# Where the sums of weight blocks stand in a fused attention and two-product kernel: two moved ahead, twelve moved back, and another room for two blocks

## The chip, the cores and the metric

The kernel runs on one core of a Trainium2 chip. The metric is the device time of one execution in microseconds (us); the median of three executions of the kernel before is 661.0 us (659.6, 661.0 and 663.91). The core has a matrix engine (TensorE, PE in the profile; its weight loads are PEld), a vector engine (VectorE, DVE), an engine for activations and copies (ScalarE, ACT), GpSimd (POOL) and SyncE (SP). In this kernel POOL and SP mostly issue transfers (DMA). Each engine works through a list of its own, in order. Those lists are laid out when the program is built.

## The reference

A causal attention with decay, in blocks of 64 positions, gives a matrix x of 3072 x 512. Behind it stands a two-layer block without bias.

```python
for b in range(nb):                                   # attention, per block of 64
    intra = einsum('bhic,bhjc->bhij', qb, kb) * Dmask
    out[:, :, sl] = einsum('bhij,bhjd->bhid', intra, vb) + einsum('bhid,bhde->bhie', qb * lam_pow, kv_state)
    kv_state = lam_block * kv_state + einsum('bhsd,bhse->bhde', kb * rev_pow, vb)

x = attn_out.transpose(0, 2, 1, 3).reshape(B * S, H * D)   # (3072, 512)
h = x @ w_in                                               # (512, 2048)
g = h - np.tanh(h)
return g @ w_out                                           # (2048, 512)
```

There are 4 batches, 8 heads, 768 positions and a head size of 64. The weights come as 64-bit floats, the rest as 32-bit floats.

## The kernel before

**Groups.** The tokens are worked on in six groups (0 to 5) of 512: 128 positions of each of the four batches. A group has an attention part, a first product (x by `w_in`, called *up*), g = h - tanh(h), and a second product (g by `w_out`, called *down*). The 2048 columns of `w_in` are four *units* u of 512 columns. The 2048 rows of `w_out` are eight *row blocks* kt of 256 rows.

**Seven products in place of eight.** Matrices are cut in 2 x 2 quarters and multiplied with seven quarter products, numbered 1 to 7 (called P1 to P7), which need sums of quarters beforehand. `sums_in(u)` (L274) makes the sums of a unit of `w_in`: four vector operations on tiles of 128 x 512, three of them into `ws[u]`, one in place into `w1[u]`. `sums_out(kt)` (L282) makes the sums of a row block of `w_out`, four vector operations of 128 x 256, and sends the block to DRAM by POOL's queue (`factors`, `fine`); `sums_fine(u)` (L298) makes a second level of sums from two row blocks and sends those too. From group 1 on, the row blocks come back from DRAM in pieces `wb` (`piece`, L746), from a ring of seven. Some products are cut a second time: `inner_weights` (L660) makes, for P2 or P4 of the first product, the sums of quarters of a unit, four vector operations of 128 x 128, into a tile of a ring of four (tag "sums") and sends them to DRAM (`fine_in`) by POOL.

**Group 0 differs.** Its first product is plain (`up_plain`, L907; matmuls at L917), since the weights arrive only then. Each weight block comes as 64-bit words into `raw64`, and `round_block` (L308) turns it into 32-bit floats with three operations on ScalarE (L318 to L320) and two on the vector engine (L322, L323). `weights(n)` rounds the next blocks; a row block kt is two of these blocks. The turns over the units run with attention of group 1 in between. Behind the last turn comes the second product of group 0, a loop over kt in which `down_first(kt, ...)` (L938; matmuls at L947) runs all seven products for one row block, into seven PSUM banks that are kept through the whole loop. Products 6 and 3 of a step need `s24`, which `sums_late(kt)` (L951; L956 and L957) makes one step ahead; products 3 to 7 need the sums of `sums_out(kt)`. `first_results` (L959) empties the banks with one ScalarE operation and seven vector operations (L963 to L972). Then group 1 starts its first product with `up(1, 0, 1)` in the banks that become free (`up`, L601; matmuls at L610).

**Where the row blocks lie meanwhile.** Row blocks 0, 1, 4 and 5 take turns in the two rooms of the pool `wst`. Blocks 2, 3, 6 and 7 borrow `ws`, the room for the sums of `w_in`: each takes a third of `ws[3]` and all of `ws[2]` (blocks 2 and 6) or `ws[1]` (blocks 3 and 7). So the sums of unit 1 can be made only when row block 7 is through, and the sums of unit 0 can be made before. After the loop the pools `stage` (with `raw64` and the rounding's addends), `qpool` and `wst` are closed, and the pools `blk` (blocks of q and k for the transposes on the vector engine, L359) and `late` (the rings `wb` and "sums") take their place.

**Group 1.** In each unit the up products run in the order 2, 6, 5, 7, 1 of the next unit, 4, 3. `sums_in(2)` and `sums_in(3)` are in units 0 and 1. In the last unit the place of product 1 is taken by P1 of the second product (`down(1, 1)`, L792; matmuls at L803). `inner_weights` runs after each unit, for P2 and P4. `pieces(g, u)` puts parts of the next group's attention after each unit: transposes, scores (L448) and masks (L455).

**What sets the order.** The list of each engine is made by a planner that takes what is ready by its own estimate of times, the earlier in the program first. `tc.keep_in_program_order` (and `tied(True, ...)`) pins an operation behind the operation written before it on its engine. The sums in the loop over kt are all pinned, with two exceptions (`sums_out` of blocks 0 and 1); so are `att_sums(1)`, `sums_in`, `inner_weights`, the transposes and the rounding. The matmuls of `down_first` and `up` are not, and neither are the tanh, the copies and the sums in `up` (L618 to L650).

Of the kernel before, what the change touches and what calls it, by code (L numbers as in the profile page):

```python
# [24 lines left out]
def kernel(  # L25
# [225 lines left out]
    def weights(n):  # L251

        while ready["done"] < min(n, len(blocks)):
            at_ = ready["done"]
            load_weights(at_ + WAHEAD)
            kind, n_, m = blocks[at_]
            if kind == "out" and m == 0:
                pair[n_] = pair_tiles(n_)
            w = w1[n_][:, m] if kind == "in" else pair[n_][m][:, 0:2]
            if at_ in wraw:  # L260
                round_block(w, wraw.pop(at_))
            else:
                load_block(nc.gpsimd, w, kind, n_, m)
            ready["done"] += 1

    def pair_tiles(kt):

        if kt % 4 > 1:
            x, y = (ws[u].rearrange("p x k c -> p (x k) c") for u in (3, 4 - kt % 4))
            return x[:, ts(kt % 4 - 2, 2)], y[:, 0:6]  # L270
        wt = wst.tile([128, 8, 256], F32, name="wt", tag="w")
        return wt[:, 0:2], wt[:, 2:8]

    def sums_in(u):  # L274
        a11, a12, a21, a22 = (w1[u][:, 2 * c:2 * c + 2, r] for r, c in ((0, 0), (0, 1), (1, 0), (1, 1)))
        s1, s2, s4 = (ws[u][:, x] for x in range(3))
        for dst, x, y, op in ((s1, a21, a22, AL.add), (s2, s1, a11, AL.subtract), (a21, a11, a21, AL.subtract),
                              (s4, a12, s2, AL.subtract)):
            tc.keep_in_program_order(nc.vector.tensor_tensor(dst, x, y, op=op))
# [285 lines left out]
    def att_sums(g, bs=None):  # L565
        x0, x1 = xt[g, 0], xt[g, 1]
        b11, b21, b12, b22 = x0[:, 0:2], x0[:, 2:4], x1[:, 0:2], x1[:, 2:4]
        tt = xpool.tile([128, 3, 2, HB], F32, name="tt", tag="tt")
        tied(g == 1, nc.vector.tensor_tensor(tt[:, 0], b12, b11, op=AL.subtract))
        tied(g == 1, nc.vector.tensor_tensor(tt[:, 1], b22, tt[:, 0], op=AL.subtract))  # L570
        tied(g == 1, nc.vector.tensor_tensor(b12, b22, b12, op=AL.subtract))
        tied(g == 1, nc.vector.tensor_tensor(tt[:, 2], b21, tt[:, 1], op=AL.subtract))
        xt[g] = dict(B11=b11, B21=b21, B22=b22, T1=tt[:, 0], T2=tt[:, 1], T3=b12, T4=tt[:, 2])
# [86 lines left out]
    def inner_weights(u, ns=INNER):  # L660
        for n in ns:
            a11, a12, a21, a22 = (a_quarter(n, u, i, k) for i in range(2) for k in range(2))
            t = late["pool"].tile([128, 4, 128], F32, name="ws2", tag="sums", bufs=4)
            s1, s2, s4 = (t[:, x] for x in range(3))
            for dst, x, y, op in ((s1, a21, a22, AL.add), (s2, s1, a11, AL.subtract), (a21, a11, a21, AL.subtract),
                                  (s4, a12, s2, AL.subtract)):
                tc.keep_in_program_order(nc.vector.tensor_tensor(dst, x, y, op=op))
            nc.gpsimd.dma_start(out=fine_in[INNER.index(n)].rearrange("x p u c -> p u x c")[:, u], in_=t[:, 0:3])
# [283 lines left out]
    def sums_late(kt):  # L952
        u, m = divmod(kt, 2)
        g11, g21, s1 = (hidden(0, c)[:, u, m] for c in (11, 21, "S1"))
        s24[kt] = work.tile([128, 2, HB], F32, name="s24", tag="th")
        tc.keep_in_program_order(nc.vector.tensor_tensor(s24[kt][:, 0], s1, g11, op=AL.subtract))  # L956
        tc.keep_in_program_order(nc.vector.tensor_tensor(s24[kt][:, 1], g21, s24[kt][:, 0], op=AL.subtract))  # L957

    def first_results():  # L959
        flat = {n: t.rearrange("q m c -> q (m c)") for n, t in acc.items()}  # L960
        q, o11, q5, o12 = (otile(x) for x in ("q1", "o11", "q5", "o12"))
        nc.scalar.activation(q, flat[1], AF.Copy)
        tc.keep_in_program_order(nc.vector.tensor_tensor(o11, q, flat[2], op=AL.add))  # L963
        store(0, 11, o11)
        tc.keep_in_program_order(nc.vector.tensor_tensor(q, q, flat[6], op=AL.add))
        tc.keep_in_program_order(nc.vector.tensor_tensor(q5, q, flat[5], op=AL.add))
        tc.keep_in_program_order(nc.vector.tensor_tensor(q, q, flat[7], op=AL.add))
        tc.keep_in_program_order(nc.vector.tensor_tensor(o12, q5, flat[3], op=AL.add))
        store(0, 12, o12)
        tc.keep_in_program_order(nc.vector.tensor_tensor(q, q, flat[4], op=AL.add))  # L970
        store(0, 21, q)
        tc.keep_in_program_order(nc.vector.tensor_tensor(q5, q5, flat[7], op=AL.add))  # L972
        store(0, 22, q5)
# [48 lines left out]
    for u, cs, n0, n1, mid, more in turns:  # L1022
        turn = up_plain(u, cs)
        if n0:
            steps(turn, KI)
            run(mid)
            weights(ready["done"] + n0)
        every(turn)
        run(more)
        weights(ready["done"] + n1)  # L1030
        if cs[-1] == 22:
            sums_first(u)
            if u == 1:
                load_weights(NU * KI)
                load(2 * B)
                powers()
            if u == 2:
                sums_in(0)
    sums_out(0)
    sums_late(0)  # L1040
    att_out(1, P1, "att")
# [3 lines left out]
    for kt in range(KH):  # L1045
        down_first(kt, (1, 2, 5, 4, 7, 6, 3) if kt + 1 < KH else (1, 2, 6, 5, 7, 3, 4))
        if kt + 1 < KH:
            sums_late(kt + 1)
        if kt + 2 < KH:
            sums_out(kt + 2)  # L1050
        if kt in (0, 1, 3, 6):
            sums_fine((kt + 1) // 2)
        if 0 < kt and kt + 3 < KH:
            weights(ready["done"] + 2)
            load_weights(ready["done"] + WAHEAD)
        if kt == 5:
            att_sums(1)
    first_results()
    sums_in(1)
    early.close()  # L1060
    late["blk"] = ctx.enter_context(tc.tile_pool(name="blk", bufs=4))
    late["pool"] = ctx.enter_context(tc.tile_pool(name="late", bufs=1))
# [20 lines left out]
    for g in range(1, NG):  # L1083
        last = g == NG - 1
        for u in range(NU):
            for n in (2, 6, 5, 7, 1, 4, 3) if g < GI else (1, 7, 3) if u == 0 else (6, 5, 1, 7, 3) if u + 1 < NU else (
                    6, 5, 7, 1, 3):
                if n != 1:
                    up(g, u, n)
                elif u + 1 < NU:  # L1090
                    up(g, u + 1, 1)
                else:
                    if g == GI - 1:
                        inner_weights(u, INNER[:1])
                        pieces(g, u)
                    every(down(g, 1))
                if g == 1 and u < 2 and n == 5:
                    sums_in(u + 2)
            if g == GI - 1:
                inner_weights(u, INNER if u + 1 < NU else INNER[1:])  # L1100
            if g >= GI or u + 1 < NU:
                pieces(g, u)
        sums_twice(g, 4)
        sums_once(g, 11, "S1", 11)
        every(down(g, 2))
        sums_twice(g, 5)
        pieces(g, "P2")
        product = down_twice(g, 4, side(g, 1))
        steps(product, 4)
        pieces(g, "P4")  # L1110
        sums_once(g, 21, 21, 11)
        sums_twice(g, 6)
        every(product)
        product = down_twice(g, 5, side(g, 0))
        steps(product, 2)
        pieces(g, "P5")
        sums_twice(g, 7)
        every(product)
        product = down_twice(g, 6, side(g, 1))
        steps(product, 2)  # L1120
        if twice(g, 3):
            sums_twice(g, 3)
        every(product)
        pieces(g, "P6")
        every(down_twice(g, 7, side(g, 0)))
        if last:
            down_end(g)
            continue
        inner_tokens(g + 1)
        p3 = down_twice(g, 3, side(g, 1)) if twice(g, 3) else down(g, 3)  # L1130
        p2 = inner_steps(g + 1, 2, "ya")
        for n, (kind, _) in enumerate(in_turn(g)):
            next(p3 if kind == "down" else p2)
            pieces(g, ("inner", n))
        every(p2)
        every(p3)
        p4 = inner_steps(g + 1, 4, "yb")
        for at_, n in enumerate((None, None, 1, None, None, 6, None, None, 5, None)):
            if n is None:
                next(p4)  # L1140
            else:
                up(g + 1, 0, n)
            pieces(g, ("end", at_))
        every(p4)
        pieces(g, "end")
# [30 lines left out]
```

## Time and profile before

| | |
|---|---|
| median of three executions | 661.0 us |
| the profiled execution | 661.42 us |
| its span, first to last instruction | 659.6 us |
| VectorE busy | 486.4 us (74%) |
| ScalarE busy | 216.7 us (33%) |
| POOL busy | 200.6 us (30%) |
| DMA | 129.14 MB, 196 GB/s over the span |
| granted TensorE clock, mean | 1.000 |

One execution is profiled. A group of the profile names a line, an engine, an operation and the tiles (`out<-in`), with the shape as partitions x elements. A wait is idle time of an engine that ended when the named operation of another engine was done. Of the span, group 0's first product lies at about 22 to 91 us, its second product at 95.7 to 145.4, group 1's first product at 145.4 to 212 (with P1 of its second product at 195.4 to 202.3), and each later group takes some 104 us. In the loop over kt, TensorE takes about 6.05 us a step.

### The profile page before, as it was taken

The page shows a single profiled execution, that of the slowest core. Times are in us where ns is not written, and L with a number is a line of the kernel's source. Part 1 is how long each engine was busy: PE and PEld are TensorE (multiplying, and loading weights), DVE is VectorE, ACT ScalarE, POOL GpSimd, SP SyncE. Part 2 cuts the span into 40 slices and gives each one's busy share as a digit, 9 for nine tenths or more (in the row PEclk, how much of TensorE's full clock was granted, in tenths as well). Part 3 has the DMA queues.
Part 4 walks back from the last instruction along what each step waited for, and adds up shares of the span by engine and source line. Part 5 has one row for each costly group of instructions (what it writes and reads, how often), then busy time and mean ns, then how long its engine had stood idle before and what let it go on. Part 6 is the DMA issues. An engine that isn't in the chain of part 4 may idle for free.

```text
span 659.6 us, 14228 instructions
## 1 busy us (share of the span) xinstructions
PE 645.3 (98%) x5632; PEld 588.5 (89%) x5632; DVE 486.4 (74%) x869; ACT 216.7 (33%) x422; POOL 200.6 (30%) x349
## 2 busy tenths in 40 slices
PE   7899999999999999999999999999999999999997
PEld 6788988888788999988999988999988899988897
DVE  4576997997977876886877787787779687357563
ACT  4767773513231223232122243112223122334110
POOL 2000246773023554001445101355202354400250
PEclk9999999999999999999999999999999999999999
DMA  9988878999729676965578865587661677600481
GB/s 214 232 189 228 233 219 284 330 317 303 161 68 248 226 244 223 198 148 141 185 235 274 189 137 146 150 291 237 197 142 68 196 239 234 215 10 1 134 287 59
DMA packets 104818, 129.14 MB, mean 196 GB/s; under 512 B 63344, under 2 KB 80880, under 8 KB 104752
## 3 DMA queue, kind: packets, MB, share of 16 engines
q0 software_dynamic: 26400, 86.27, 41.2%
q1 hardware_dynamic: 78208, 41.96, 27.5%
q8 instruction: 45, 0.74, 0.5%
q14 instruction: 21, 0.17, 0.1%
q10 hardware_dynamic: 144, 0.00, 0.0%
HBM read 108.01 MB, written 20.19 MB: 194 GB/s over the span
## 4 chain that ended last, share of the span: by engine, by line
PE 79%; DVE 6%; DMA 6%; SPq 3%; issue 3%; ACT 1%; POOL 1%; DVEq 0%; POOLq 0%; ACTq 0%
PE y L610 15%; PE y L858 13%; PE zw L858 10%; PE z L610 9%; PE h L917 6%; PE y L803 5%; PE y L694 4%; PE w L803 4%; DMA k_blk<-in_k_dram 3%; PE z L694 2%; PE sp L448 2%; SPq L156 2%; PE acc L947 2%; DMA fine<-f 1%; PE op L484 1%
## 5 line engine op out<-in xcount | busy, mean ns | idle before, releaser
L767 POOL DMA_DIRECT2D wb<-fine x168 | 90.7, 540 | 156.7 <-PE y L858 53.0
L618 ACT ACTIVATE th<-g 128x512 f32<-128x512 f32 x76 | 47.5, 630 | 117.4 <-DVE g L623 48.9
L610 PE MATMUL y<-xt,w 128*128 128x256 f32 x320 | 74.0, 382 | 1.1 <-ACT g L638 1.1
L619 DVE TENSOR_TENSOR g<-g,th 128x512 f32<-128x512 f32 x76 | 52.4, 691 | 23.2 <-ACT th L618 22.8
L861 ACT ACTIVATE q<-y 128x128 f32<-128x128 f32 x96 | 26.7, 278 | 130.3 <-PE y L858 128.9
L610 PEld LDWEIGHTS y<-xt,w 128*128 128x128 f32 x320 | 59.8, 190 | 10.7 <-ACT g L638 2.7
L858 PE MATMUL y<-wb,g 128*128 128x128 f32 x456 | 60.2, 277 | 0.0
L917 PE MATMUL h<-xt,w 128*128 128x256 f32 x256 | 57.5, 381 | 2.4 <-DVE w L323 1.2
L917 PEld LDWEIGHTS h<-xt,w 128*128 128x128 f32 x256 | 47.8, 190 | 9.5 <-DVE ss L455 1.3
L770 POOL DMA_DIRECT2D wb<-factors x44 | 23.8, 543 | 106.2 <-PE y L803 70.2
L858 PEld LDWEIGHTS y<-wb,g 128*128 128x128 f32 x456 | 55.1, 192 | 0.6
L858 PE MATMUL zw<-wb,g 128*128 128x128 f32 x304 | 40.3, 275 | 0.2 <-DVE o L827 0.2
L610 PE MATMUL z<-xt,ws 128*128 128x256 f32 x160 | 37.9, 380 | 1.0 <-DVE g L641 1.0
L610 PE MATMUL y<-tt,ws 128*128 128x256 f32 x160 | 37.8, 379 | 0.0
L610 PE MATMUL z<-tt,ws 128*128 128x256 f32 x160 | 37.8, 379 | 0.0
L858 PEld LDWEIGHTS zw<-wb,g 128*128 128x128 f32 x304 | 37.0, 192 | 0.4 <-DVE o L827 0.4
L803 PE MATMUL y<-wb,g 128*128 128x256 f32 x160 | 35.4, 379 | 0.0
L803 PE MATMUL w<-wb,g 128*128 128x256 f32 x160 | 35.3, 379 | 0.0
L610 PEld LDWEIGHTS z<-xt,ws 128*128 128x128 f32 x160 | 30.3, 190 | 5.5 <-DVE g L641 1.4
L803 PEld LDWEIGHTS y<-wb,g 128*128 128x128 f32 x160 | 30.4, 190 | 4.1
L803 PEld LDWEIGHTS w<-wb,g 128*128 128x128 f32 x160 | 30.4, 190 | 4.1
L610 PEld LDWEIGHTS y<-tt,ws 128*128 128x128 f32 x160 | 30.1, 190 | 3.9
(188 smaller groups left out, 1293.8 us busy)
## 6 DMA issues: line engine op xcount, KB each, us to landing
wb<-fine POOLq DMA_DIRECT2D x168, 256.0 KB, 3.6
wb<-factors POOLq DMA_DIRECT2D x44, 256.0 KB, 4.4
wb<-fine_in POOLq DMA_DIRECT2D x24, 256.0 KB, 3.8
raw<-in_moe_w_out_dram POOLq DMA_DIRECT2D x10, 512.0 KB, 5.5
raw<-in_moe_w_in_dram SPq DMA_DIRECT2D x8, 512.0 KB, 6.1
raw<-in_moe_w_in_dram SPq DMA_DIRECT2D x16, 256.0 KB, 6.2
fine<-f POOLq DMA_DIRECT2D x16, 256.0 KB, 5.6
q_blk<-in_q_dram SPq DMA_DIRECT2D x32, 128.0 KB, 3.8
```

The source lines that it names most:

```text
L156: nc.sync.dma_start(out=x, in_=src[b, :, ts(g, BLK), :].rearrange("h s d -> s h d")))
L448: tied(True, nc.tensor.matmul(out=dst, lhsT=keys(p, j, late_), rhs=qt[ts(j, 64), p, rows], start=True, stop=True))
L610: nc.tensor.matmul(out=t[:, m, :], lhsT=wt[:, kt, ts(m, 128)], rhs=x[:, kt, :], start=first and m == 0 and kt == 0, stop=kt == 1, skip_gro ...
L618: nc.scalar.activation(th, src, AF.Tanh)
L619: nc.vector.tensor_tensor(dst(c), src, th, op=AL.subtract)
L694: nc.tensor.matmul(out=dst[:, ts(u, 128)], lhsT=a, rhs=b, start=x in (1, 2, 5) and u == 0, stop=True, skip_group_check=True)
L767: nc.gpsimd.dma_start(out=t.rearrange("p m c -> p (m c)"), in_=fine[TWICE.index(n_), SUB.index(x_)].rearrange("p u c -> p (u c)"))
L770: nc.gpsimd.dma_start(out=t, in_=factors[XAT[FACT[n_][1]]][:, 2 * x_:2 * x_ + 2, :])
L803: nc.tensor.matmul(out=t[:, m, :], lhsT=a[:, u, kt, ts(m, 128)], rhs=wb[:, kt, :], start=first and u == 0 and m == 0 and kt == 0, stop=u = ...
L858: nc.tensor.matmul(out=dst, lhsT=a[:, u, :], rhs=wb[:, ts(u, 128)], start=x in (1, 2) and u == 0, stop=u == NU - 1, skip_group_check=True)
L861: nc.scalar.activation(keep, dst, AF.Copy)
L917: tied(u == 0, nc.tensor.matmul(out=hm[c][:, m, :], lhsT=w1[u][:, i, a, ts(m, 128)], rhs=xt[0, t][:, i, :], start=m == 0 and i == 0, stop= ...
```

## The change

Three things move; no operation is added or taken away.

- `sums_in(0)` goes from the end of the turn of unit 2 in group 0's first product into the second product, at kt = 4, behind `att_sums(1)`, which comes from kt = 5. `sums_in(1)` goes from behind `first_results` to the end of kt = 6, ahead of `first_results`.
- Row blocks: block 3 borrows `ws[0]` in place of `ws[1]`, and block 7 takes a room of `wst`, the one that block 4 had. Its rounding goes from kt = 4 to kt = 5, right before its `sums_out`.
- In group 1, `inner_weights` for P4 of units 0, 1 and 2 goes from behind these units to the place right before `down(1, 1)` in the last unit, behind `pieces(1, 3)`, which changes places with `inner_weights` for P2 of unit 3.

```diff
     def pair_tiles(kt):
-        if kt % 4 > 1:
-            x, y = (ws[u].rearrange("p x k c -> p (x k) c") for u in (3, 4 - kt % 4))
-            return x[:, ts(kt % 4 - 2, 2)], y[:, 0:6]
+        if kt in (2, 3, 6):
+            x, y = (ws[u].rearrange("p x k c -> p (x k) c") for u in (3, 0 if kt == 3 else 2))
+            return x[:, ts(kt % 2, 2)], y[:, 0:6]
         wt = wst.tile([128, 8, 256], F32, name="wt", tag="w")
         return wt[:, 0:2], wt[:, 2:8]
...
                 powers()
-            if u == 2:
-                sums_in(0)
...
         if kt + 1 < KH:
             sums_late(kt + 1)
+        if kt == 5:
+            weights(ready["done"] + 2)
         if kt + 2 < KH:
             sums_out(kt + 2)
         if kt in (0, 1, 3, 6):
             sums_fine((kt + 1) // 2)
-        if 0 < kt and kt + 3 < KH:
+        if 0 < kt < 4:
             weights(ready["done"] + 2)
             load_weights(ready["done"] + WAHEAD)
-        if kt == 5:
+        if kt == 4:
             att_sums(1)
+            sums_in(0)
+        if kt == 6:
+            sums_in(1)
     first_results()
-    sums_in(1)
...
                     if g == GI - 1:
+                        pieces(g, u)
                         inner_weights(u, INNER[:1])
-                        pieces(g, u)
+                        for x in range(u):
+                            inner_weights(x, INNER[1:])
                     every(down(g, 1))
...
             if g == GI - 1:
-                inner_weights(u, INNER if u + 1 < NU else INNER[1:])
+                inner_weights(u, INNER[:1] if u + 1 < NU else INNER[1:])
```

## The prediction, on record before the changed kernel ran

> **What bounds the kernel now.** I read the page's first part, then TensorE's waits, then windows by stage, then the vector engine's timeline.
>
> ```profile
> PE 645.3 (98%) x5632; PEld 588.5 (89%) x5632; DVE 486.4 (74%) x869; ACT 216.7 (33%) x422; POOL 200.6 (30%) x349
> ```
>
> TensorE is busy for 645.3 of 659.6 us, and the change gives it no matmul more or less. So only its idle time can go, 14.3 us, and most of that lies in the first 30 us and in the tail after 650. Between 60 and 260 us, where the change works, its waits are these (total, times, longest):
>
> ```profile
> PE h L917 <- DVE ss L455: 1.2, 1, 1.2
> PE y L610 <- ACT g L638: 1.1, 1, 1.1
> PE z L610 <- DVE g L641: 1.0, 1, 1.0
> PE acc L947 <- DVE s L956: 0.7, 2, 0.4
> PE sp L448 <- DVE kt L359: 0.6, 1, 0.6
> ```
>
> That is 4.6 us, and the most that can be won: 0.7%. The vector engine (DVE) ends all of it, the second through ScalarE. The windows show where DVE has no room (columns: stretch, its length, then PE, PEld, DVE, ACT, POOL busy, clock, DMA share, GB/s):
>
> ```profile
> 75.00:95.00 20.00, 18.82 (x314) 16.48 (x312) 19.66 (x42) 13.67 (x24) 8.15 (x13) 1.00 0.68 210
> 95.00:132.00 37.00, 36.27 (x198) 31.28 (x195) 31.14 (x73) 18.73 (x31) 24.98 (x37) 1.00 0.95 302
> 132.00:154.00 22.00, 20.88 (x97) 18.07 (x96) 20.51 (x42) 3.48 (x6) 17.38 (x27) 1.00 1.05 319
> 165.00:177.00 12.00, 10.43 (x101) 8.63 (x103) 12.00 (x24) 2.39 (x5) 1.53 (x2) 1.00 0.71 157
> 195.00:212.00 17.00, 17.00 (x80) 14.98 (x79) 11.94 (x23) 3.05 (x5) 6.28 (x11) 1.00 0.98 226
> ```
>
> DVE is full at 75 to 95, at 132 to 154 and at 165 to 177, and has 5 us free at 195 to 212. Its timeline gives the prices:
>
> ```profile
> 76.58 0.69 DVE L279 TENSOR_TENSOR ws<-w 128x512 f32<-128x512 f32 x1
> ...
> 79.11 1.29 DVE L372 TENSOR_TENSOR qd<-qt,fwd 128x512 f32<-128x512 f32 x2
> ...
> 133.26 0.42 DVE L322 TENSOR_SCALAR ws<-ws 128x512 uint32<-128x512 uint32 x1
> ...
> 135.59 0.42 DVE L956 TENSOR_TENSOR s<-gS,g 128x256 f32<-128x256 f32 x1
> ...
> 144.39 0.68 DVE L963 TENSOR_TENSOR o<-q,acc 128x512 f32<-128x512 f32 x1
> ...
> 149.16 0.68 DVE L279 TENSOR_TENSOR ws<-w 128x512 f32<-128x512 f32 x1
> ...
> 151.70 0.68 DVE L635 TENSOR_TENSOR g<-g,w 128x512 f32<-128x512 f32 x1
> ```
>
> From start to start: four sums of one unit 2.53 us (76.58 to 79.11), the rounding of a row block pair 2.33 (133.26 to 135.59), the seven sums of the first results 4.77 (144.39 to 149.16). From the same timeline: sums_late 0.79, sums_out 1.47, sums_fine 3.21, att_sums 2.53, four inner sums 0.81.
>
> **The change part by part.** I count in the clock of the old run and subtract at the end what was won earlier.
>
> 1. *sums_in(0) leaves 76.58.* 2.53 us of DVE go. What follows is held by ScalarE: its rounding result at 78.67, its second tanh at 80.22. So the second L925 ends near 80.9 instead of 82.76, and L529, three L285 and the first L455 end near 83.2 instead of 84.86. TensorE is ready at 83.71: its wait of 1.18 us goes. No more is won, since ScalarE's next work waits for TensorE's L512 (82.63), which is not moved. From here all is 1.18 us earlier: **-1.18**.
>
> 2. *Other rooms.* Block 3 takes unit 0's ws instead of unit 1's, which only has to be over before sums_in(0); its last product ends at 120.55, its stores are issued by 112.92. Block 7 takes the ring room of block 4, so its rounding (6 ACT, 4 DVE instructions) goes from kt 4 to kt 5. The raw loads on SP are already all asked for at kt 3 in both: nothing moves there. The room is free when block 4's last product (126.59), its fine store (issued at 121.24, median 5.4 to land) and sums_fine(2) (128.6) are through; ScalarE had to wait until 129.95 for the addend anyway and ends at 133.2, DVE asks at 139. Cost nothing, with 5 us of cover. Behind it on POOL, block 7's four stores come later, and prefetches of wb that now wait for this room stand before result stores; the prefetches are first used at 195.43, and nobody needs the stores' tiles before 202.
>
> 3. *The queue of DVE in the second product.* All these operations are pinned in program order. After sums_out(6) at 133.26 now come att_sums(1) to 135.79, sums_in(0) to 138.32, sums_late(6) with its first result at 138.74 (before 136.01), rounding 7 to 141.44, sums_out(7) to 142.91, sums_late(7) with its first result at 143.33, to 143.71, sums_fine(3) to 146.92, sums_in(1) to 149.45, first results to 154.22, then L635 (before 151.70: +2.52, the four sums that came in). TensorE wants s24 of kt 6 at 137.62 and gets it at 138.79: 1.17 us. kt 7 starts at 140.51, is 0.13 short at its second product and 1.02 at the third, and ends at 147.7 instead of 145.39. Bank w is let go by L963, now behind sums_in(1), at 150.13, where TensorE asks at 149.4: 0.8. The fifth product of the next stage, begun at 153.58 behind ScalarE's L638, then begins at 155.4. If ScalarE keeps its tanh (L618, which waits for L635) ahead of that copy, as it did, it begins at 156.1. **+1.8 to +2.5**. Which of the two, the list of instructions will decide. It put the tanh first though its input came 1.8 us after the copy's, so it took DVE to be earlier than it was; 2.5 us more work may turn that round. I take the middle, +2.15.
>
> The row says the sums cost the same among POOL's issues: L303 takes 688 ns at 128x512 there, L279 took 684 to 692. [...]
>
> 4. *Inner weights.* Of 32 small sums, 12 (units 0 to 2 of P4, 0.81 us a unit) go from 166, 182 and 194 into P1 at 195 to 205, with three DMAs of 0.76 us on POOL. Only unit 0's lie ahead of the waits at 172.95 (0.97) and 176.36 (0.59), with DVE full from 164.8: **-0.82**. If DVE is not the pace there but the blocks' landings, 0; if all follows, -1.56. In P1, DVE idles 3.09 us before 204.95; transposes come first, then 4 x 0.81, so it just fits. The ring of four tiles "sums" makes the fifth wait for its store: landing 2.8 us, POOL's loads in front wait for TensorE, at most 4.64 us. Product 4 reads s2 at 218.59 and it was ready at 212: hidden.
>
> Sum: -1.18 + 2.15 - 0.82 = +0.15 us on the profiled 661.42 (span 659.6 and 1.8 around it); on the median of 661.0, **661.2**.
>
> **Rivals.**
> - *A: the sums fit.* If the list fills TensorE's gaps at kt 6 and 7 with other products (5 and 7 need only sums_out), the copy goes first on ScalarE and bank w is free in time, the wait of 1.12 goes too: -1.18 - 1.12 - 0.82, with 1.56 for the last: -3.1 to -3.9, **657.1 to 657.9**. For it: these products are not pinned. Against: 20.51 of 22 us of DVE are taken.
> - *B: slower, the landings pace DVE.* At 109 to 116 DVE waits 3.4 us for stores of f tiles (landing 6.08 and 3.55 us in the chain of waits), with a DMA share of 0.95. If they land no earlier, the 1.18 is lost at kt 2, and sums and rounding behind it stand as in step 3: +1.8 to +2.5, less 0.82 or nothing: **662.0 to 663.5**. It decides if these waits grow by more than 0.6 us.
> - *C: slower, block 7's room.* Rounding stands right before its use. If block 4's store lands after about 133, each further us goes to TensorE and to all pinned behind it: from 5 us late, **666 and more**. Against: 5 us of cover. The granted clock is 1.00 around every wait so far, the longest in this part 1.18 us. [...]
> - *D: it does not do what it says*: the unpinned work is listed anew elsewhere and waits move anywhere.
>
> **How the numbers follow.** Forecast (660.5 to 662): 0.45. A 0.22, B 0.20, C 0.07, D 0.06. The range reaches from A's low end to B with 1.5 us for what the medians scatter (659.6 to 663.91): 657 to 665. Over 1%, about what a measurement of this kernel can tell from no change, is 6.6 us: no case gains it, since only 4.6 us are there, so faster has 0.03 for D and scatter; slower has C and part of D, 0.09; within it 0.88.
>
> **What would show it.** Right: L917 <- DVE ss L455 gone; new waits of L947 for L956 of about 1 us each at kt 6 and kt 7; DVE busy 95 to 132 unchanged and no idle at 132 to 154; PE z L610 <- DVE g L641 under 0.3; no new wait at 195 to 215; PE busy 645. A: no wait over 0.5 us at kt 6 and 7. B: DVE f L303 <- DMA over 4 us. C: ACT L318 waits for a DMA or DVE L323 for ACT. Wrong altogether: a wait outside 75 to 215 us that is over 1 us longer.

## The result, and the profile after

The changed kernel takes 669.7 us in the median (668.34 to 671.08, four executions) against 660.8 of the kernel before beside it: the ratio is 1.0127, with a 95% interval of 1.0084 to 1.0171. It is slower by 8.9 us, where 661.2 was forecast and the range ended at 665. The profiled execution took 668.66 us, its span 666.8, 7.2 more than before.

TensorE's waits between 60 and 260 us come first again (total, times, longest), and ahead of them the busy time of the whole span:

```profile
PE 649.1 (97%) x5632; PEld 590.3 (89%) x5632; DVE 487.8 (73%) x869; ACT 216.2 (32%) x422; POOL 199.8 (30%) x349
```

```profile
PE zw L858 <- DVE o L827: 5.3, 1, 5.3
PE acc L947 <- DVE s L956: 2.4, 4, 1.0
PE sp L448 <- DVE kt L359: 0.5, 2, 0.3
PE w L610 <- DVE o L963: 0.5, 1, 0.5
PE y L610 <- ACT g L638: 0.5, 1, 0.5
```

From the second line on stand the waits of the part in which the change works, 3.9 us in all. The first one is new, is longer than everything that there was to win, and lies at 217.9 to 223.2 us, behind the part in which anything was moved. The windows by stage (length, busy time of each engine, clock, DMA share, GB/s):

```profile
132.00:154.00 22.00, 19.82 (x89) 16.07 (x87) 20.69 (x40) 1.68 (x3) 14.94 (x22) 1.00 0.99 304
165.00:177.00 12.00, 11.96 (x56) 10.19 (x54) 10.71 (x20) 3.88 (x7) 0.76 (x1) 1.00 0.21 59
195.00:212.00 17.00, 17.00 (x81) 14.96 (x80) 9.29 (x18) 3.05 (x5) 4.03 (x8) 1.00 0.78 193
220.00:225.00 5.00, 1.78 (x8) 1.78 (x9) 4.96 (x7) 0.00 (x0) 0.33 (x1) 0.77 0.11 34
225.00:230.00 5.00, 5.00 (x42) 5.00 (x41) 4.76 (x8) 0.56 (x2) 3.49 (x7) 0.89 0.77 220
```

At 165 to 177 TensorE no longer waits (11.96 of 12 us busy, before 10.43). At 195 to 212 DVE was meant to fill its 5 idle us with 12 small sums, and is busy for less than before (9.29, before 11.94). At 220 to 230 the granted clock is 0.77 and 0.89, where it was 1.00 in the kernel before:

```profile
220.00:230.00 10.00, 10.00 (x92) 10.00 (x92) 9.83 (x16) 1.67 (x6) 6.10 (x12) 1.00 0.83 273
```

The starts of the stages divide the loss:

| from one start to the next, us | before | after | difference | predicted |
|---|---|---|---|---|
| start of the span to second product of group 0 | 95.67 | 94.24 | -1.43 | -1.18 |
| to P1 of group 1's second product (first L803) | 99.76 | 101.26 | +1.50 | +1.33 |
| to product 4 of it (first L858) | 21.28 | 21.28 | 0 | 0 |
| to the next group's first up product (first L694) | 29.25 | 36.71 | +7.46 | 0 |
| to the end of the span | 413.6 | 413.3 | -0.3 | 0 |

The first row also holds TensorE's waits for the first loads, which differ from one profile to the next: those for `k_nat` and `v_nat` add to 1.5 us in the kernel before and to 2.0 in e1 below, and the changed kernel's profile lists none. The part that was worked out step by step came to +0.07 us, and the whole loss is in one stage, to which the prediction gave nothing. DVE's timeline there (start, duration, line, tiles, shapes; idle time ahead and its releaser in brackets), first in the kernel before:

```profile
200.78 1.09 DVE L359 STREAM_TRANSPOSE kt<-k_blk 128x512 f32<-128x512 f32 x1
204.95 0.69 DVE L619 TENSOR_TENSOR g<-y,th 128x512 f32<-128x512 f32 x1 [3.09 <-ACT th L618]
...
208.88 0.69 DVE L650 TENSOR_TENSOR g<-g,g 128x512 f32<-128x512 f32 x1
209.49 0.28 DVE L667 TENSOR_TENSOR ws<-w 128x128 f32<-128x128 f32 x1
...
214.63 0.68 DVE L827 TENSOR_TENSOR o<-q,w 128x512 f32<-128x512 f32 x1
```

and in the changed kernel:

```profile
208.95 0.69 DVE L650 TENSOR_TENSOR g<-g,g 128x512 f32<-128x512 f32 x1
209.56 1.10 DVE L359 STREAM_TRANSPOSE kt<-k_blk 128x512 f32<-128x512 f32 x1
210.51 0.27 DVE L667 TENSOR_TENSOR ws<-w 128x128 f32<-128x128 f32 x1
...
214.02 0.28 DVE L667 TENSOR_TENSOR ws<-w,ws 128x128 f32<-128x128 f32 x1
217.28 0.29 DVE L667 TENSOR_TENSOR ws<-w 128x128 f32<-128x128 f32 x1 [2.98 <-DMA fine_in<-ws]
...
218.22 0.69 DVE L837 TENSOR_TENSOR s<-g 128x512 f32<-128x512 f32 x1
...
220.21 2.35 DVE L789 TENSOR_TENSOR g<-gS,g 128x1024 f32<-128x1024 f32 x2
222.48 0.68 DVE L827 TENSOR_TENSOR o<-q,w 128x512 f32<-128x512 f32 x1
```

L827 empties the bank that TensorE takes next. It had started at 214.63 and starts 7.85 us later. Between L650 and L827 stand now 20 small sums (L667), where only the four of P4 of unit 3 stood before; the 16 others are pinned behind the k transpose of the last batch, and that transpose, which ran at 200.78 before, is listed behind L650, at 209.56. So the small sums start at 210.51 instead of about 201, and the fifth tile of their ring of four waits 2.98 us for a store. The transfers issued at 211 to 219 us (line and queue, issues, KB each, median us from issue to landing) show what it waits for:

```profile
fine_in<-ws POOLq DMA_DIRECT2D x5, 192.0 KB, 4.7
```

The first of these stores is issued at 212.30, 0.79 us after its tile is done. Ahead of 205.02, where the sums were meant to run, DVE idles 4.66 us. TensorE behind the wait:

```profile
216.78 1.16 PE L858 MATMUL y<-wb,g 128*128 128x128 f32 x8
223.22 2.08 PE L858 MATMUL zw<-wb,g 128*128 128x128 f32 x8 [5.28 <-DVE o L827]
225.09 1.57 PE L858 MATMUL y<-wb,s 128*128 128x128 f32 x8
226.49 1.06 PE L858 MATMUL zw<-wb,s 128*128 128x128 f32 x8
```

Eight matmuls take 0.89 us from start to start where the clock is full; these two groups take 1.87 and 1.40. The wait makes 223.22 of what would have been 217.77, 5.45 us; the slow groups add 0.98 and 0.51. With a wait of 0.16 for `wb` that is 7.10 of the 7.46; 0.36 was not followed.

### The profile page after: what moved, and what is told of

It reads as the page before. It is cut to its first block, busy times and chain, and to the rows that moved or that the text cites. A ratio compares the mean times of both kernels' runs of the same rounds, so it can differ in the third digit from the quotient of the medians.

```text
span 666.8 us, 14230 instructions
## 1 busy us (share of the span) xinstructions
PE 649.1 (97%) x5632; PEld 590.3 (89%) x5632; DVE 487.8 (73%) x869; ACT 216.2 (32%) x422; POOL 199.8 (30%) x349
## 4 chain that ended last, share of the span: by engine, by line
PE 78%; issue 6%; DVE 5%; DMA 4%; POOL 3%; SPq 2%; ACT 1%; POOLq 0%; DVEq 0%; ACTq 0%
PE y L610 16%; PE y L858 11%; PE z L610 10%; PE zw L858 9%; PE h L917 7%; PE y L803 5%; PE y L694 4%; PE w L803 4%; PE z L694 2%; PE sp L448 2%; DMA fine<-f 1%; PE op L498 1%; POOL wb L767 1%; PE op L484 1%; DMA wb<-fine 1%
## 5 line engine op out<-in xcount | busy, mean ns | idle before, releaser
L858 PE MATMUL y<-wb,g 128*128 128x128 f32 x456 | 60.3, 277 | 0.0
L917 PE MATMUL h<-xt,w 128*128 128x256 f32 x256 | 57.5, 381 | 1.4 <-DVE w L323 1.4
L858 PEld LDWEIGHTS y<-wb,g 128*128 128x128 f32 x456 | 55.1, 192 | 0.7
L917 PEld LDWEIGHTS h<-xt,w 128*128 128x128 f32 x256 | 47.8, 190 | 8.4 <-DVE w L323 1.3
L858 PE MATMUL zw<-wb,g 128*128 128x128 f32 x304 | 41.3, 280 | 5.7 <-DVE o L827 5.5
L858 PEld LDWEIGHTS zw<-wb,g 128*128 128x128 f32 x304 | 37.8, 196 | 6.2 <-DVE o L827 5.9
L803 PE MATMUL y<-wb,g 128*128 128x256 f32 x160 | 35.4, 379 | 0.0
L803 PE MATMUL w<-wb,g 128*128 128x256 f32 x160 | 35.3, 379 | 0.0
L803 PEld LDWEIGHTS y<-wb,g 128*128 128x128 f32 x160 | 30.4, 190 | 4.1
L803 PEld LDWEIGHTS w<-wb,g 128*128 128x128 f32 x160 | 30.4, 190 | 4.1
L610 PEld LDWEIGHTS z<-tt,ws 128*128 128x128 f32 x160 | 30.1, 190 | 3.9
```

The source lines that it names most:

```text
L610: nc.tensor.matmul(out=t[:, m, :], lhsT=wt[:, kt, ts(m, 128)], rhs=x[:, kt, :], start=first and m == 0 and kt == 0, stop=kt == 1, skip_gro ...
L803: nc.tensor.matmul(out=t[:, m, :], lhsT=a[:, u, kt, ts(m, 128)], rhs=wb[:, kt, :], start=first and u == 0 and m == 0 and kt == 0, stop=u = ...
L858: nc.tensor.matmul(out=dst, lhsT=a[:, u, :], rhs=wb[:, ts(u, 128)], start=x in (1, 2) and u == 0, stop=u == NU - 1, skip_group_check=True)
L917: tied(u == 0, nc.tensor.matmul(out=hm[c][:, m, :], lhsT=w1[u][:, i, a, ts(m, 128)], rhs=xt[0, t][:, i, :], start=m == 0 and i == 0, stop= ...
```

## The experiments

The theory from these lines, called *queue* below: the third part of the change puts 16 small sums behind the pieces of unit 3, and a list in which the last k transpose stands late holds them until DVE's idle time is over. The rivals were the second product, the ring of tiles by itself, the late transposes by themselves, and, for the size, something else than the wait behind the low clock.

### The third part undone: e1_inner_back

```diff
                     if g == GI - 1:
-                        pieces(g, u)
                         inner_weights(u, INNER[:1])
-                        for x in range(u):
-                            inner_weights(x, INNER[1:])
+                        pieces(g, u)
...
-                inner_weights(u, INNER[:1] if u + 1 < NU else INNER[1:])
+                inner_weights(u, INNER if u + 1 < NU else INNER[1:])
```

> The changed kernel with the third part undone: inner_weights for P2 and P4 stand behind each unit again; the moved sums and the other rooms stay. Theory (queue): the loss comes from 16 small sums of P4 and P2 that are pinned behind a late transpose in the last unit of group 1, and hold up sums_twice(1, 4) and L827, which frees the bank of zw. Then TensorE's wait for L827 (5.28 us) and the low clock behind it are gone: 661 to 663 us, ratio to the kernel before 1.000 to 1.004. Rival (second product): the moved sums and rooms themselves are what costs, and the wait at 223 is only where it comes due: 667 us or more, ratio 1.009 or more.

662.46 us, ratio 1.0018 (1.0007 to 1.0029). TensorE doesn't wait for L827 at 218.69, where it takes the bank. The rival of the second product falls. What is left, +1.2 us, is the price of the first two parts, which the prediction had put at -1.18 + 2.15 = +0.97.

### The same sums ahead of the pieces: e2_inner_first

```diff
                     if g == GI - 1:
-                        pieces(g, u)
                         inner_weights(u, INNER[:1])
                         for x in range(u):
                             inner_weights(x, INNER[1:])
+                        pieces(g, u)
```

> The changed kernel with one change of order: in the last unit of group 1 the small sums (P2 of unit 3, P4 of units 0 to 2) stand ahead of pieces(1, 3), the transposes of batch 3, not behind. Theory (queue): they then run at about 198 to 205, in VectorE's idle time; no wait of TensorE for L827: 661 to 662.5 us, ratio 1.000 to 1.003. Rival (ring): what costs is the ring of four tiles, whose fifth user waits for a store whatever the order: VectorE still waits about 3 us for fine_in and TensorE some 2 to 5 us: 664 to 669 us.

661.57 us, ratio 1.0002 (0.9992 to 1.0012): the place of one line decides 8 us. DVE's timeline shows that the small sums, no longer pinned behind that transpose, run in the idle time, with no wait for a store, though the last k transpose is as late as in the changed kernel:

```profile
199.32 0.28 DVE L667 TENSOR_TENSOR ws<-w 128x128 f32<-128x128 f32 x1
...
203.65 0.28 DVE L667 TENSOR_TENSOR ws<-w,ws 128x128 f32<-128x128 f32 x1
...
209.96 0.69 DVE L650 TENSOR_TENSOR g<-g,g 128x512 f32<-128x512 f32 x1
...
211.50 1.10 DVE L359 STREAM_TRANSPOSE kt<-k_blk 128x512 f32<-128x512 f32 x1
...
216.64 0.68 DVE L827 TENSOR_TENSOR o<-q,w 128x512 f32<-128x512 f32 x1
```

L827 is done at 217.32 and TensorE takes the bank at 218.78, 1.46 us later. The ring was not too small; it was used too late. The median is 0.9 us below that of the run above, but the intervals (1.0007 to 1.0029 and 0.9992 to 1.0012) overlap, and the traces give the third part only 0.21 of it: from the start of the fifth product of group 1 to P1 it is 41.03 us in the run above and 40.82 here, as in the changed kernel.

### A fifth tile: e3_ring5

The changed kernel with `bufs=5` for the tiles "sums" and, for the room, six instead of seven in the ring of `wb`.

> The changed kernel with five tiles in the ring of the small sums in place of four, and six wb pieces in place of seven to make room. Theory (queue): the start of the small sums at 210.5 stays, only VectorE's wait of 2.98 us for a store goes; TensorE's wait for L827 falls from 5.28 to about 2.3 us and, being short, leaves the clock at 1.00: 668.7 - 3.0 - 1.5 = 664.2 us, ratio 1.005 (six pieces may cost up to 1 us more elsewhere). Rival (ring): the store is the cause, and the wait goes wholly: 661.5 us, ratio 1.001. If the store is of no account: 668 us or more.

672.5 us, ratio 1.0175 (1.0159 to 1.0191): missed by 8 us. The wait did not go, it moved to the next user of the ring:

```profile
218.34 0.69 DVE L837 TENSOR_TENSOR s<-g 128x512 f32<-128x512 f32 x1 [1.81 <-DMA fine_in<-ws]
```

TensorE still waits 3.83 us for L827, and the clock still falls (0.68 on average at 222 to 227 us). About 3.2 us more come later, from the first L694 to the end (416.5 against 413.3 us), where one piece of `wb` less is kept ahead; which wait they are was not followed up.

### The third part alone: e4_inner_only

The kernel before with the third part of the diff and nothing else.

> The kernel before with the third part of the change alone (P4's small sums of units 0 to 2 before down(1, 1), behind pieces(1, 3)). In the list of this build the transposes of batch 3 stand 16 places earlier than in the changed kernel, ahead of the tanh of product 4. Theory (queue): the 16 small sums run at about 201 to 205 in VectorE's idle time, no wait for L827; the waits at 173 and 176 shrink by 0.8 us: 660.2 us, ratio 0.9975 to 1.000. Rival (moving small sums into P1 costs in itself, by the ring or by POOL): a wait for L827 of 2 us or more, 663 us or more.

662.32 us, ratio 1.0018 (1.0006 to 1.0031), where the theory expected at most 1.000. There is no wait for L827: the transposes have their old places (the last k at 200.72). So the third part alone doesn't make the loss. Nor does it bring the 0.82 us here: the list puts transposes and L372 into the freed time, and TensorE's waits at 173 to 178 grow, 2.1 us against 1.56 before.

```profile
PE z L610 <- DVE g L641: 1.2, 1, 1.2
PE y L610 <- ACT g L638: 1.1, 1, 1.1
PE sp L448 <- DVE kt L359: 1.0, 1, 1.0
```

### The wait by itself: e5_wait6 and e6_wait11

The version of e2 with one sum done 7 times (e5) and 12 times (e6, where the 7 below is a 12). The added line moves the later lines down by one, so L859 is the L858 of the other runs:

```diff
         s1, s2 = (late["pool"].tile([128, NU, 128], F32, name=f"s{x}", tag="sums", bufs=4) for x in (1, 2))
-        hold(s1, a21, a22, op=AL.add)
+        for _ in range(7 if (g, n) == (1, 4) else 1):
+            hold(s1, a21, a22, op=AL.add)
```

> The version with the inner sums ahead of the pieces (661.6 us), in which one operation of DVE, the first of the three sums of product 4 of group 1, is done seven times instead of once; it writes the same values each time. Each repeat takes 0.6 us on DVE (sums of the same line start 0.61 to 0.78 us apart) and stands ahead of L827, which lets go of the bank that TensorE takes at 218.8; L827 had been done 1.4 us before. So TensorE should wait 6 x 0.605 - 1.4 = 2.2 us for L827 and for nothing else. Theory (the granted clock falls only after a wait of more than 3 us): clock 1.00 behind the wait, the eight matmuls behind it 0.9 us each group as before, time 661.6 + 2.2 = 663.8 us. Rival (every wait of some us costs as much again, in proportion: 7.5 for 5.3 in the changed kernel): 661.6 + 3.1 = 664.7 us and a granted clock under 0.95 in the 5 us behind it.

> The same with eleven repeats: TensorE should wait 11 x 0.605 - 1.4 = 5.2 us for L827, as long as in the changed kernel, and with nothing else of the changed kernel's late transposes and store waits in it. Theory (the long wait itself lowers the clock, and the two make the whole loss): granted clock under 0.9 in the 5 us behind the wait, the way from L858's start to the first L694 longer by 5.2 + about 2 us, time 661.6 + 7.2 = 668.8 us, near the changed kernel's 669.7. Rival (the low clock of the changed kernel came from something else, such as its transfers): clock 1.00, 661.6 + 5.2 = 666.8 us.

e5 takes 666.36 us (ratio 1.0093, 1.0070 to 1.0115), 4.8 more than e2 by the medians, and more than both forecasts. A repeat took 0.73 us on DVE, not 0.605, so that TensorE waits 2.80 us. The 3 us of the theory, the author's estimate, lay between the 1.18 us that had left the clock at 1.00 (before) and the 3.83 us with which it had fallen (e3); with 2.80 us it fell too, as the rival had it. The rival's price in proportion to the wait does not hold in the trace: the two groups of matmuls behind the wait start at 219.93 and 221.79, the next one at 223.21: that is 1.50 us more than two groups take at full clock, against 1.49 behind the wait of 5.28 us. TensorE's wait, and windows of 1 us of e5 (the clock is the third number from the end):

```profile
PE zw L859 <- DVE o L827: 2.8, 1, 2.8
```

```profile
218.00:219.00 1.00, 0.00 (x0) 0.00 (x0) 1.00 (x2) 0.00 (x0) 0.00 (x0) 1.00 0.00 0
219.00:220.00 1.00, 0.07 (x1) 0.08 (x1) 1.00 (x3) 0.00 (x0) 0.00 (x0) 0.73 0.00 0
220.00:221.00 1.00, 1.00 (x5) 1.00 (x6) 0.96 (x2) 0.00 (x0) 0.00 (x0) 0.50 0.00 0
221.00:222.00 1.00, 1.00 (x6) 1.00 (x6) 0.80 (x2) 0.00 (x0) 0.63 (x1) 0.50 0.00 0
222.00:223.00 1.00, 1.00 (x8) 1.00 (x7) 0.96 (x2) 0.00 (x0) 1.00 (x3) 0.56 0.36 127
223.00:224.00 1.00, 1.00 (x12) 1.00 (x11) 1.00 (x3) 0.28 (x1) 0.50 (x2) 1.00 0.79 193
```

A value of 0.73 is counted as 0.54 us of that window at 0.50, as in the windows behind it, and the rest at 1.00. Added up from 219 on, the clock is at 0.50 for 0.54 + 1 + 1 + 0.88 = 3.42 us. The same sum over windows of 1 us gives 3.40 in the changed kernel, 3.40 in e3, and twice as much, 6.84, in e6; over windows of 5 us it gives 6.8 in e10 below. The low stretch starts 2.3 us after TensorE fell idle in e5, 4.8 in the changed kernel. Between the wait of 2.80 us in e5 and that of 5.28 in the changed kernel its length does not grow (3.42 and 3.40 us).

e6 takes 670.2 us (1.0153, 1.0131 to 1.0174), 8.6 more than e2, against 7.2 expected by the theory and 5.2 by its rival: a late L827, with only the old four small sums behind L650 and no wait of DVE for a store, goes with a loss as large as the change's and with a low clock (0.50 from 221 to 227 us). It is no clean copy, since TensorE's list was laid out anew: its idle time is spread over several waits, the longest of 3.00 us, 1.5 us of it is for `wb`, and the clock was at 0.50 for 6.84 us.

### One room undone: e7_block7_ws1

The changed kernel, in which block 7 borrows `ws[1]` again and `sums_in(1)` therefore stands behind `first_results()`.

> The changed kernel with one room undone: block 7 borrows unit 1's ws again, as before, and so sums_in(1), whose result lies there, goes back behind the first results. The inner weights stay where the change put them, behind the pieces of unit 3. Theory (where block 7's rounding gets its room decides where the list puts the transposes of group 1's last unit, and these decide the wait): as built, two k transposes stand ahead of the small sums again; the small sums run at 199 to 206, wait for no store ahead of product 4's sums, L827 is done before TensorE asks, wait under 0.5 us; the second product loses the waits for bank w (0.5) and some of the next stage: 660.3 to 662.5 us. Rival (the small sums behind the pieces are late by themselves, whatever the transposes): the fifth of their tiles waits for its store, L827 after 219, TensorE waits over 2 us: 664 us or more.

662.63 us, ratio 1.0031 (1.0017 to 1.0046), just above the expected 660.3 to 662.5. The inner weights stand where the change put them, and TensorE doesn't wait for L827. One of product 4's sums still waits 1.61 us for a store, against the expectation, but L827 is done 0.6 us before TensorE takes the bank. The k transpose is early again, and the small sums follow it:

```profile
200.20 1.09 DVE L359 STREAM_TRANSPOSE kt<-k_blk 128x512 f32<-128x512 f32 x1
201.13 0.29 DVE L667 TENSOR_TENSOR ws<-w 128x128 f32<-128x128 f32 x1
```

### Block 7's room alone, and with the third part: e9_room7 and e10_room7_inner

The kernel before with this, and the second run with the third part of the diff besides:

```diff
-        if kt % 4 > 1:
+        if kt in (2, 3, 6):
             x, y = (ws[u].rearrange("p x k c -> p (x k) c") for u in (3, 4 - kt % 4))
```

> The kernel before with one edit: block 7 takes a room of the ring of converted blocks in place of unit 1's ws. No sum and no inner weight is moved. Theory (this room decides how the list lays the transposes of group 1's last unit; it does harm only where 16 small sums more stand behind them): as built, the last k transpose stands behind L650, as in the changed kernel, but only four small sums lie behind L650. L827 had 2.4 us to spare in the kernel before and the transpose takes 0.94, so TensorE does not wait for it; the waits at 172 to 177 (1.56) shrink to about 0.5: 660 to 661 us. Rival (the late transposes alone hold product 4 up): TensorE waits over 2 us for L827 and the clock falls, 664 us or more.

> The kernel before with two edits: block 7's room as in the run above, and the third part of the change, the inner weights behind the pieces of unit 3. The first part, the sums inside the second product, is left out. Theory (room and third part together make the whole loss, each alone none): the small sums start behind L650 at about 210.5, the fifth tile waits about 3 us for its store, TensorE waits 4.5 to 5.5 us for L827, the granted clock is under 0.9 in the 5 us behind, 667.5 to 669.5 us. Rival (the moved sums of the first part are needed for it, by the time they cost DVE): wait under 1 us, 663 us or less.

e9 takes 660.01 us, ratio 0.9985 (0.9975 to 0.9996): faster, by a little. The last k transpose is late as in the changed kernel, but only four small sums are behind L650, and L827 starts in time:

```profile
209.43 1.10 DVE L359 STREAM_TRANSPOSE kt<-k_blk 128x512 f32<-128x512 f32 x1
...
214.57 0.68 DVE L827 TENSOR_TENSOR o<-q,w 128x512 f32<-128x512 f32 x1
```

The wait for L641 (1.0) is gone, and that for the transposes is 0.5.

e10 takes 669.97 us, ratio 1.0137 (1.0119 to 1.0156), as much as the whole change, with none of its moved `w_in` sums. The wait is longer than the expected 4.5 to 5.5 us, and the time a little above the expected range:

```profile
PE zw L858 <- DVE o L827: 6.0, 1, 6.0
```

```profile
216.45 0.29 DVE L667 TENSOR_TENSOR ws<-w 128x128 f32<-128x128 f32 x1 [3.61 <-DMA fine_in<-ws]
```

So the loss needs two parts. The room alone is -0.15%, the inner weights alone +0.18%, both together +1.4%.

### Ways to a faster kernel: e8_gap, e11_late1, e12_best

All three start from the kernel before. e8 moves one call; e11 adds to that; e12 is e11 with the edit of e9.

```diff
-            if u == 2:
-                sums_in(0)
...
         if kt + 2 < KH:
             sums_out(kt + 2)
+        if kt == 1:
+            sums_in(0)
...
     first_results()
-    sums_in(1)
...
-                if g == 1 and u < 2 and n == 5:
+                if g == 1 and u == 0 and n == 6:
+                    sums_in(1)
+                if g == 1 and u < 2 and n == 7:
                     sums_in(u + 2)
```

(The first two places are e8, the last two are what e11 adds.)

> The kernel before with one edit: sums_in(0) is not done at 76.6, in unit 2 of group 0, but at kt 1 of the second product, where DVE waits 3.35 us for stores of fine tiles at 109 to 116. Theory (its 2.53 us cost only where DVE is full): TensorE's wait of 1.18 for the scores' copy L455 goes, DVE's waits for the stores shrink by 2.5 and nothing behind moves: 661.0 - 1.2 = 659.8 us. Rival (start of the second product earlier, but the stores land when they land and rounding paces it): the 1.2 us come back as waits of L947 at kt 2 or 3, 661.0 us.

> The kernel of 660.0 us with sums_in(0) in DVE's idle time at kt 1, and one edit more: sums_in(1) is not done behind the first results but behind up(1, 0, 6), and sums_in(2) and sums_in(3) two products later than before. DVE then reaches L635 2.5 us earlier. Theory: TensorE's wait of 1.1 us for ScalarE's L638 goes, that for L641 (0.9) shrinks by half: 658.4 us. Rival (DVE is the pace from 164 to 178, and sums that come later make its waits there longer): 659.8 us or more.

> The run above, and block 7 in a room of the ring, as in the changed kernel; the inner weights stay as before. Theory (with the inner weights at their old places the room's list is harmless, and its spread transposes leave TensorE about 1 us less to wait at 172 to 177): 657.9 us, no wait over 0.6 us between 60 and 260. Rival (the rounding of block 7 or the late transposes cost as much again): 659 us or more.

e8: 659.99 us, ratio 0.9985 (0.9972 to 0.9998). The wait of 1.18 for L455 is gone, and DVE's waits for the stores of `f` shrank from 3.35 us to one of 0.60, so the sums lie where DVE had nothing to do. The gain, about 1 us (0.1 to 1.9 by the interval), agrees with the term of -1.18; the waits of 0.7 for L956 are gone here too.

e11: 660.07 us, ratio 0.9979 (0.9967 to 0.9991). Both waits named are gone, 2.0 us in all, but 1.2 came back as a longer wait for the transposes (1.8 in place of 0.6) and 0.7 at L947: the rival's number. DVE's work moved into the stretch in which it is full. A wait of 1.0 us for `wb` in a later group is new as well, and seven of its twelve executions have a lower granted clock (0.996 or 0.997), of which more in the section behind the experiments.

```profile
PE sp L448 <- DVE kt L359: 1.8, 1, 1.8
PE acc L947 <- DVE s L956: 0.7, 2, 0.4
```

e12: 658.18 us (656.9 to 658.62), ratio 0.9950 (0.9937 to 0.9963), the fastest, and faster than both kernels. With the transposes spread by block 7's room, what is left of waits between 60 and 260 us is 1.3 us, of 4.6 before (the longest is 0.7, where at most 0.6 was expected):

```profile
PE sp L448 <- DVE kt L359: 1.1, 2, 0.7
PE acc L947 <- DVE s L956: 0.2, 1, 0.2
```

## Why the prediction was wrong, and where it was right

**Step 1, -1.18: right.** The wait of L917 for L455 is gone. From the last but one group of L917's matmuls to the last it is 7.67 us in the changed kernel and in e8, 8.92 before; e8, which moves these four sums alone, gains 0.15%, about 1 us. The -1.43 of the table proves less, since it holds the first loads too.

**Step 2, other rooms at no cost: right for what it looked at, and half of the cause.** Block 7's rounding had its room in time: ScalarE's first operation of it waited for sums_fine(2) to let go of the room, but DVE and TensorE did not wait for the rounding. The step priced the room by data alone: who waits for it, and until when. It did not ask what else the list does when a room is given back at another time. e9 shows that this room alone moves the last k transpose from 200.78 to 209.43, and the transposes before it too. Nor was the room free of effect where it did no harm: it gains about 1 us by itself.

**Step 3, +1.8 to +2.5: right.** The waits for s24 were predicted at 1.17 in kt 6, and 0.13 and 1.02 in kt 7; measured 1.02 and 0.67. Bank w: predicted 0.8, measured 0.50. In the clock of the old run (1.43 us added) the next stage starts at 147.8 (predicted 147.7) and its fifth product at 156.1, the upper of the two values named; ScalarE's tanh did stay ahead of the copy. The sum had taken the middle, 2.15; measured up to this fifth product it is +2.5. From the second product to P1 the difference was +1.50, against 2.15 - 0.82 = +1.33, but that this agrees is in part luck, as step 4 shows.

**Step 4, -0.82, "it just fits", "hidden": the step that failed.** The gain did not come from the inner weights. From the fifth product to P1 it is 41.85 us before, 41.03 with the room and without the inner weights (e9 and e1), 40.82 with room and inner weights (changed kernel, e2 and e10), and 42.40 with the inner weights alone (e4). So the room brought the 0.82 by moving the transposes, and the inner weights brought 0.21 on top of it and nothing without it; that the table shows about the predicted number is luck. The cover was not there. "In P1, DVE idles 3.09 us before 204.95; transposes come first, then 4 x 0.81" took the place of the transposes from the trace of before and assumed that it stays. It was this that the room changed: the last transpose came behind L650, all that is pinned behind it came after the idle time, and the wait for the ring's store, which the step knew of and called hidden, lay on the way to L827 (a landing was put at 2.8 us; the median of the five stores is 4.7). The step looked at product 4, which reads `s2`; it did not look at L827, which stands behind these sums in DVE's list and frees TensorE's bank.

**The rivals.** None named this. D ("the unpinned work is listed anew elsewhere and waits move anywhere") is the nearest, at 0.06, with no place and no price; what moved was not even unpinned, since a pin fixes only the order among pinned operations, and the free ones, L650 here, may be listed on either side. A and B did not come: kt 6 and 7 had waits of 1.02 and 0.67, and the waits for the stores of f tiles stayed at 3.3 us. C had a long wait of TensorE for a late store, and put it at another room; that the granted clock was 1.00 around the waits of the kernel before, of 1.18 us at most there, did not carry over to one of 5.28 us. The sign that the prediction named for a failure, a new wait outside 75 to 215 us that is over 1 us longer, is what came.

**The clock.** The forecast has no term for it. The stretches at 0.50 measure 3.40 us in the changed kernel, 3.40 in e3 and 3.42 in e5, with waits of TensorE of 5.28, 3.83 and 2.80 us; they measure 6.84 us in e6, where the longest wait is 3.00, and 6.8 in e10, where it is 6.02. Against the same groups of matmuls at full clock, the low clock took 0.98 + 0.51 = 1.49 us in the changed kernel, 1.50 in e5 and 1.7 in e3 (three groups in 4.41 us, from 223.28 to 227.69).

The clock does not fall in every execution of a kernel. One of the four executions of e5 has a granted clock of 1.000 over the whole (665.19 us, the others 0.997 and 665.46 to 667.72). A wait of 1.75 us (e11, for the transposes) left the clock at 1.00 in the profiled execution; but seven of e11's twelve executions have 0.996 or 0.997, as the profiled one of the changed kernel has 0.997, and their median is 1.5 us above that of the other five (660.95 and 659.41). Where their clock fell no trace shows. And two of the four executions of the changed kernel have 0.995 and take some 2.4 us more than the other two; that their clock was low for 6.8 us, as in e10 at 0.995, was not traced.

**Open.** Why the planner lists the transposes later when block 7 lies in `wst` was not shown. `wst` makes room for the pool of q and k blocks, so an estimate that the room comes free later would do it; but the loads of these blocks were really asked for at about the same time in e9 (145.1 to 157.3 us, before 144.6 to 158.9), and earlier in the changed kernel (140.2 to 154.5).

## What to carry to other kernels

When operations are moved behind others that are pinned, ask for each neighbour what pins it and what may be listed between them; the idle time that the old trace shows belongs to the old list, and a change of a buffer can lay that list out anew far from where it was made. Follow a moved operation to everything behind it on its engine, above all to what frees a bank for the critical engine, and not only to the readers of its own result. Put work into idle time that a pinned wait creates, as in e8, rather than into time that the list happens to leave.

## What the runs showed of the hardware

Five profiles have a wait of TensorE of 2.8 us or more between 60 and 260 us (the changed kernel 5.28, e3 3.83, e5 2.80, e6 3.00, e10 6.02), and in each the granted clock fell during it or just behind it: to 0.50 for 3.4 us in the first three, which took 1.5 us in the changed kernel and in e5 and 1.7 in e3, and for 6.8 us in e6 and e10. It is not certain in each execution: one of four executions of e5 has a clock of 1.000, and seven of twelve of e11, whose longest traced wait there is 1.75 us, have 0.996 or 0.997. In e5 and e6 the same sum of DVE (128x512), repeated on the same output tile, started every 0.73 us; in the changed kernel a sum that neither reads nor rewrites what the one before it wrote started 0.61 us behind it (219.00 to 219.61).
